# A fused dynamic convolution and token-routed MLP: a finer ring for x, and the selection of tokens in two rounds

## Chip, cores and metric

One core of one Trainium2 chip runs the whole program. The metric is the device time of one execution in microseconds (us); the profile adds a trace of one execution.

## What is computed

```python
# x (8, 4160, 192) fp32, weight_gen (8, 4160, 8 heads, 7 taps), capacity 128
w = exp(weight_gen - max over taps);  w = w / (sum over taps + 1e-9)
x_pad = 6 rows of zeros ahead of each batch of x
out[b, s, h] = sum over k of w[b, s, h, k] * x_pad[b, s + k, h]      # h: 24 columns
# then, for each batch b, on y = out:
scores = y[b] @ w_gate
top_idx = the 128 rows with the largest scores
xe = y[b, top_idx];  ye = relu(xe @ w1) @ w2                         # 192 -> 1024 -> 192
out[b, top_idx] = xe + sigmoid(scores[top_idx])[:, None] * ye
```

So there is a weighted sum of seven neighbouring rows with weights of its own for each row and head, and then a small MLP on the 128 best rows of each of the 8 batches, added back to those rows.

## The kernel before

The 33,280 rows are cut into tiles of 56 output rows (7 times 8), held on 64 partitions with the 6 rows ahead; two half ranges of a group of tiles share the 128 partitions. Four tiles are a pair (224 rows); there are NPR = 149 pairs and NS = 75 conv steps of two pairs each. A step is 32 matmuls (`conv`, L728), two halves by eight heads for each pair, with a banded 128x112 matrix as weights. VectorE builds that matrix (`band`, L707) from the transposed softmax weights, two steps ahead of its use, in NB = 3 buffers. ScalarE copies the sums out of PSUM one step later (`evac`, L742; two PSUM buffers `cps`), and SP's queue stores them.

The softmax weights come in NG = 5 groups of 32 pairs (16 steps): load, exp, sum, reciprocal, product (`sm_exp` to `sm_norm`, ScalarE and VectorE, in two halves of a group, the product at L242 and L252), then four transposes of quarters (`wt_t`, L267) whose copies (`wt_c`, L277 or L279) give `wts`. Where a batch begins inside a group, L252 multiplies by an edge mask that GpSimd makes (`edge_mask`, L796).

x lies in a ring of NX = 6 buffers of CP = 8 pairs (sixteen tiles on each partition half), loaded by GpSimd's queue (`load_x`, L166, two DMAs a piece; a buffer is loaded again when all its conv steps are emitted). The half of the buffer that holds no data must be zero, and GpSimd writes those zeros once (`zero_x`, L776 and L777).

The scores are not taken from the output: dot products of the rows of x with w_gate, head by head, are weighted by the softmax weights. A unit of eight tiles of x is transposed on TensorE (`y_unit_a`, L300, 24 instructions), copied by ScalarE and VectorE (`y_unit_c`, L308 and L309, tile `xT`), multiplied by `gmat` (`y_unit_b`, L321 to L327) and, piece by piece, cast to `y` by VectorE (`y_unit_d`, L335). There are 38 units, spread evenly over steps 0 to 57: unit k at step 58k/38, rounded down. After the last unit of a group `sc_moves` forms its scores (`score_t` to `score_r`; the product at L371 on VectorE, the sum by matmuls L386), writes them to DRAM (`sc_d`, L404) and reads back those of every batch that is complete (`scores`, L411), both on GpSimd's queue, which also carries the loads of x.

When the last group has its scores (about step 66), the selection runs once for all batches: candidates per partition (`sel_cand`), their values broadcast through DRAM (`cand_d` L481, `bc` L482), 24 rank counts, half on ScalarE and half on VectorE (`sel_rank`), 24 one-hot matrices on VectorE (`sel_hot`, L538) each with a matmul (L542), and the row numbers (`sel_fin`). Then GpSimd gathers the rows of all eight batches from the output in DRAM (`ex_gather`, L624), TensorE, ScalarE and VectorE run the MLP of one batch after another (`ex_k` to `ex_s`; the last operation is `ye`, L685), and GpSimd scatters each result (L690).

The order of all this is written out by hand in two lists per step: `reads` (emitted ahead of the step's matmuls) and `plan` (behind them). `at(s, f)` and `rd(s, f)` put a call there. Each engine works through its own instructions in that order, so an instruction that waits holds all that stand behind it on the same engine.

Of the kernel before, what the change touches and what calls it, by code (L numbers as in the profile page):

```python
# [18 lines left out]
P = 128  # L19
# [11 lines left out]
CP = 8  # L31
# [66 lines left out]
def fast_path(  # L98
# [18 lines left out]
    NX = 6  # L117
# [4 lines left out]
    wrb = [consts.tile([P, 4 * M, HK], FP32, name=f"wr{i}") for i in range(2)]  # L122
# [26 lines left out]
    def load_x(c):  # L149
        t = xb[c % NX].rearrange("p c k i d -> p c (k i) d")  # L150
        gi, l = divmod(c * CT, 2 * GP)
        for cc in range(2):
# [6 lines left out]
            while first + (hi - 1) * HB + R > N:  # L159
                hi -= 1  # L160
                f = first + hi * HB
                if f + K - 1 < N:
# [3 lines left out]
            nc.gpsimd.dma_start(  # L166
                out=t[R * cc:R * cc + R, cc, lo:hi, :],
                in_=ap_of(x_flat, x_flat.offset + (first + lo * HB) * D,
                          [[D, R], [HB * D, hi - lo], [1, D]]),
            )  # L170
# [117 lines left out]
    ybank = ps_y.tile([P, 2, CT, H], FP32, name="ybank")  # L288
    YT = 8
    YR = YT * D // P  # L290

    def y_unit_a(c, u):
        nr = min(YR, ntile(c) * D // P - u * YR)
        xf = xb[c % NX].rearrange("p c k i d -> p c (k i d)")
        tps = [ps_t.tile([P, 16, R], FP16, tag="tps", name=f"xtps{cc}") for cc in range(2)]
        for r in range(nr):
            for cc in range(2):
                ps = slice(R * cc, R * cc + R)
                o = (u * YR + r) * P
                nc.tensor.transpose(  # L300
                    out=tps[cc][:, r, :], in_=xf[ps, cc, o:o + P], identity=ident16[ps, ps]
                )
        ystate[(c, u)] = (tps, nr)

    def y_unit_c(c, u):
        tps, nr = ystate.pop((c, u))
# [3 lines left out]
        ystate[(c, u)] = xT  # L310

    def y_unit_b(c, u):
        nr = min(YR, ntile(c) * D // P - u * YR)
        nt = nr * P // D
        xT = ystate.pop((c, u))
        yps = ybank[:, c % 2, u * YT:u * YT + nt, :]
# [13 lines left out]
    def y_unit_d(c):  # L330
        nt = ntile(c)
        gi, l = divmod(c * CT, 2 * GP)
        if l == 0:
            ygr[gi] = ypl.tile([P, H, R], FP16, tag="y16", name="y16")
        nc.vector.tensor_copy(  # L335
            out=ygr[gi][:, :, l:l + nt].rearrange("p h t -> p t h"), in_=ybank[:, c % 2, 0:nt, :]
# [42 lines left out]
    def score_m(gi, odd):  # L379
        n = P  # L380
        sp = sps_.pop((gi, odd))
        if odd == 0:
            scs[gi] = ps_t.tile([P, 2, M // 2, Q, 8], FP32, tag="tps", name="sps")
        sps = scs[gi]
        for h in range(H):
            nc.tensor.matmul(  # L386
                out=sps[0:n, odd].rearrange("p m q k -> p m (q k)"), lhsT=ident16[0:n, 0:n],
                rhs=sp[0:n, :, h, :], start=(h == 0), stop=(h == H - 1), skip_group_check=True,
            )

    def score_r(gi):
        n = P
        sps = scs[gi]
        sc = smp.tile([P, Q, M // 2, 2], FP32, tag="sc", name="sc")
        nc.vector.tensor_reduce(  # L395
            out=sc[0:n].rearrange("p q m o -> p o m q"), in_=sps[0:n, :, :, :, 0:K],
            axis=AX.X, op=ALU.add,
        )
        parts = ((0, P, half_of(gi, 0, 0)),)
        if ntiles(gi) < R:  # L400
            parts = tuple((R * cc, ntiles(gi), half_of(gi, cc, 0)) for cc in range(2))
        for p0, n, h0 in parts:
            n = min(n, NHF - h0)
            nc.gpsimd.dma_start(  # L404
                out=sc_d[h0:h0 + n, :], in_=sc[p0:p0 + n].rearrange("p q m o -> p (q m o)")
            )
        beg = half_of(gi, 0, 0) * HB
        end = min(beg + 2 * ntiles(gi) * HB, N)
        for b in range(B):
            if beg < (b + 1) * S <= end:  # L410
                nc.gpsimd.dma_start(  # L411
# [23 lines left out]
    sel_i = selp.tile([P, B], I32, name="sel_i")  # L435
    gates = selp.tile([P, B], FP32, name="gates")
# [5 lines left out]
    def sel_consts():  # L442
        it = selp.tile([P, P], I32, name="it_i")
        nc.gpsimd.iota(out=it[:, :], pattern=[[1, P]], base=0, channel_multiplier=0)
        nc.gpsimd.tensor_copy(out=iota_f[:, :], in_=it[:, :])
# [34 lines left out]
    def sel_bcast():  # L480
        nc.gpsimd.dma_start(out=cand_d[:, :], in_=cv[:, :])  # L481
        nc.gpsimd.dma_start(  # L482
# [46 lines left out]
    def sel_hot(k):  # L529
        if k < ACT_K and k % 3 == 0:  # L530
            nc.vector.tensor_scalar(
                out=rank[:, k:k + 3], in0=rank[:, k:k + 3], scalar1=float(NR - 1), scalar2=0.5,
                op0=ALU.add, op1=MUL,
            )
        if k == 0:
            selst["ps"] = ps_t.tile([P, B, NV], FP32, tag="tps", name="lps")
        oh = ohp.tile([P, P], FP16, tag="oh", name="oh")
        nc.vector.tensor_scalar(  # L538
            out=oh[:, :], in0=iota_f[:, :], scalar1=rank[:, k:k + 1], scalar2=None,
            op0=ALU.is_equal,  # L540
        )
        nc.tensor.matmul(  # L542
            out=selst["ps"][:, :, :], lhsT=oh[:, :], rhs=rhs[:, k], start=(k == 0),
            stop=(k == CAND - 1),
        )

    def sel_fin():
        nc.scalar.copy(out=lists[:, :, :], in_=selst["ps"][:, :, :])
# [69 lines left out]
    NXE = B  # L618
    xebuf = [consts.tile([CAP, D], FP32, name=f"xe{i}_") for i in range(NXE)]

    def ex_gather(b):
        xe = xebuf[b % NXE]
        nc.gpsimd.memset(tick[:, :], 0.0)
# [58 lines left out]
    def ex_s(b):  # L682
        xe, yps = est[b][0], est[b][-1]
        ye = exq.tile([CAP, D], FP32, tag="ye", name="ye")
# [78 lines left out]
    nc.vector.memset(a_view(0)[:, :, :, K], 0.0)  # L763
    nc.vector.memset(amem[0][:, M * H * HB:], 0.0)
    nc.vector.memset(emax[:, :], 0.0)
    nc.vector.memset(rmax[:, :], 0.0)
# [8 lines left out]
    def zero_x(i):  # L775
        nc.gpsimd.memset(xb[i][R:P, 0], 0.0)  # L776
        nc.gpsimd.memset(xb[i][0:R, 1], 0.0)  # L777
# [26 lines left out]
    nc.gpsimd.tensor_copy(out=landed[:, 0:1], in_=wrb[0][:, 0, 0:1])  # L804
    load_x(0)
    zero_x(0)
    nc.gpsimd.tensor_copy(out=landed[:, 1:2], in_=wrb[1][:, 0, 0:1])
    load_x(1)
    load_x(2)
# [6 lines left out]
    zero_x(1)  # L816
    load_x(3)
    load_x(4)
# [14 lines left out]
    load_x(5)  # L833
    for i in range(3, NX):
        zero_x(i)
    sm_exp(0, 0)
# [29 lines left out]
    Y_END = 58  # L866
# [287 lines left out]
```

## Time and profile before

| | before |
|---|---|
| three runs | 289.55, 290.39, 288.17 us; median 289.55 |
| the profiled execution | 288.73 us, its span in the trace 286.9 us |
| busy: TensorE, VectorE | 173.8 us (61%), 184.7 us (64%) |
| busy: ScalarE, GpSimd | 149.6 us (52%), 108.3 us (38%) |
| mean granted TensorE clock | 0.747 of full speed |

Times below are us from the start of the span. PE is TensorE, PEld its weight load, DVE VectorE, ACT ScalarE, POOL GpSimd; GpSimd's DMA issues count as busy in its rows. A row of a table by stretch gives for each engine its busy time and, in brackets, the number of its instructions. The conv steps begin at 20.0 (step 0), 55.2 (step 8), 95.4 (step 20), 162.1 (step 42), 205.0 (step 56) and 229.0 (step 69); the first gather starts at 252.3.

### The profile page before, as it was taken

How to read it: one execution, taken by the hardware profiler on the slowest of the kernel's cores; microseconds unless marked ns; L12 is line 12 of the kernel's file. 1: busy time of each engine (PE TensorE's matmuls, PEld its weight loads, DVE VectorE, ACT ScalarE, POOL GpSimd, SP SyncE). 2: the span in 40 equal slices, each digit the busy share in tenths (PEclk: the TensorE clock that was granted, in tenths of full speed). 3: DMA queues.
4: the chain of work that ended last, by engine and by line, in shares of the span. 5: the costliest groups of instructions: out<-in, count | busy, mean ns of one | idle time of the engine just before them, and what ended most of it. 6: DMA issues, size and time to landing. Idle time of an engine off the chain costs nothing.

```text
span 286.9 us, 10859 instructions
## 1 busy us (share of the span) xinstructions
PE 173.8 (61%) x4759; PEld 158.4 (55%) x4759; DVE 184.7 (64%) x304; ACT 149.6 (52%) x234; POOL 108.3 (38%) x156
## 2 busy tenths in 40 slices
PE   0065480278667685777776894758978033738860
PEld 0065480178556684777676684748878032637740
DVE  4878050685648996456887753979797589824540
ACT  3527190077646497455676574686775129422420
POOL 5999999996020130203302030500103010077550
PEclk9999576556859959597555797768999855555996
DMA  6999995199999999998999999996487603342110
GB/s 224 201 232 211 221 210 152 6 180 238 228 287 275 250 162 232 186 280 260 200 236 176 265 170 219 142 240 188 112 227 212 196 29 99 98 114 76 43 45 17
DMA packets 78910, 51.22 MB, mean 179 GB/s; under 512 B 43402, under 2 KB 77181, under 8 KB 78858
## 3 DMA queue, kind: packets, MB, share of 16 engines
q0 software_dynamic: 41312, 17.44, 48.1%
q1 hardware_dynamic: 37546, 33.03, 39.8%
q8 instruction: 39, 0.64, 0.8%
q14 instruction: 13, 0.11, 0.1%
HBM read 39.35 MB, written 26.49 MB: 229 GB/s over the span
## 4 chain that ended last, share of the span: by engine, by line
PE 33%; issue 23%; POOL 17%; DVE 12%; DMA 10%; ACT 2%; POOLq 0%; DVEq 0%; ACTq 0%
PE cps L728 13%; POOL xb L776 6%; PE xtps L300 5%; POOL xb L777 5%; DMA xb<-in_x_dram 4%; POOL xb L166 4%; PE wtps L267 4%; DVE band L707 4%; DMA sc_d<-sc 4%; PE sps L386 3%; PE hps L661 3%; PE yeps L678 2%; DMA wr<-in_weight_gen_dram 2%; DVE amem L242 1%; DVE sp L371 1%
## 5 line engine op out<-in xcount | busy, mean ns | idle before, releaser
L728 PE MATMUL cps<-xb,band 128*128 128x48 f16 x2384 | 91.6, 199 | 44.1 <-DVE band L707 21.7
L728 PEld LDWEIGHTS <-band 128*128 128x128 f16 x2384 | 83.3, 107 | 48.8 <-issue 23.2
L707 DVE TENSOR_TENSOR band<-wts,mask 128x1792 f16<-128x1792 f16 (+1 forms) x75 | 83.4, 1124 | 2.7 <-PE cps L728 2.6
L742 ACT COPY co<-cps 112x768 f32<-112x768 f32 (+1 forms) x75 | 59.0, 792 | 48.4 <-PE cps L728 42.6
L166 POOL DMA_DIRECT2D xb<-in_x_dram x38 | 31.1, 829 | 57.3 <-PE cps L728 45.7
L309 DVE COPY xT<-xtps 128x768 f16<-128x768 f16 (+1 forms) x38 | 20.7, 545 | 42.5 <-PE xtps L300 28.2
L308 ACT COPY xT<-xtps 128x768 f16<-128x768 f16 (+1 forms) x38 | 29.9, 788 | 11.8 <-PE xtps L300 7.3
L300 PE MATMUL xtps<-ident,xb 64*128 64x64 f16 x894 | 26.9, 216 | 9.4 <-issue 7.1
L267 PE MATMUL wtps<-ident,amem 64*64 64x64 f16 x640 | 16.8, 214 | 18.2 <-DVE amem L242 13.9
L300 PEld LDWEIGHTS <-xb 64*128 64x128 f16 x894 | 20.9, 111 | 11.5 <-issue 7.8
L267 PEld LDWEIGHTS <-amem 64*64 64x64 f16 x640 | 15.0, 128 | 20.0 <-DVE amem L242 13.9
L279 ACT COPY wts<-wtps 128x1024 f16<-128x1024 f16 x18 | 18.3, 1015 | 13.8 <-PE wtps L267 13.7
L321 PE MATMUL ybank<-gmat,xT 128*128 128x8 f16 x149 | 15.4, 169 | 11.4 <-POOL gmat L828 6.2
L404 POOL DMA_DIRECT2D sc_d<-sc x6 | 3.4, 566 | 45.7 <-DVE sc L395 45.7
L242 DVE TENSOR_TENSOR amem<-amem,r 128x2048 f16<-128x2048 f16 (+1 forms) x10 | 10.9, 1093 | 13.4 <-POOL edge L796 13.3
L210 ACT ACTIVATE amem<-wr 128x1792 f16<-128x1792 f32 (+1 forms) x10 | 15.2, 1515 | 7.4 <-DVE amem L252 3.7
L324 PEld LDWEIGHTS <-xT 128*128 128x128 f16 x149 | 12.8, 102 | 11.2 <-issue 11.2
L221 DVE TENSOR_REDUCE den<-amem 128x256 f32<-128x1792 f16 (+1 forms) x10 | 17.7, 1776 | 1.6 <-ACT amem L210 1.6
L777 POOL MEMSET xb<- 64x3072 f16 x6 | 15.9, 2652 | 0.3
L776 POOL MEMSET xb<- 64x3072 f16 x6 | 15.9, 2653 | 0.2
L324 PE MATMUL ybank<-gmat,xT 128*128 128x16 f16 x149 | 15.3, 172 | 0.6 <-POOL gmat L828 0.6
L335 DVE CAST y<-ybank 128x128 f16<-128x128 f32 (+1 forms) x19 | 13.6, 717 | 3.1 <-PE ybank L327 2.9
(164 smaller groups left out, 254.2 us busy)
## 6 DMA issues: line engine op xcount, KB each, us to landing
out_dram<-co SPq DMA_DIRECT2D x148, 168.0 KB, 5.8
xb<-in_x_dram POOLq DMA_DIRECT2D x35, 384.0 KB, 10.0
wr<-in_weight_gen_dram SPq DMA_DIRECT2D x4, 896.0 KB, 5.8
wr<-in_weight_gen_dram SPq DMA_DIRECT2D x4, 672.0 KB, 4.2
wr<-in_weight_gen_dram SPq DMA_DIRECT2D x2, 224.0 KB, 6.9
w_sb<-in_moe_w_dram POOLq DMA_DIRECT2D x1, 384.0 KB
xb<-in_x_dram POOLq DMA_DIRECT2D x1, 360.0 KB
wr<-in_weight_gen_dram SPq DMA_DIRECT2D x2, 168.0 KB
```

Of the source, the lines that this page charges most:

```text
L166: nc.gpsimd.dma_start(out=t[R * cc:R * cc + R, cc, lo:hi, :], in_=ap_of(x_flat, x_flat.offset + (first + lo * HB) * D, [[D, R], [HB * D, h ...
L267: nc.tensor.transpose(out=tp[ps, hh, m, :], in_=am[ps, o:o + R], identity=ident16[ps, ps])
L279: nc.scalar.copy(out=dst, in_=src)
L300: nc.tensor.transpose(out=tps[cc][:, r, :], in_=xf[ps, cc, o:o + P], identity=ident16[ps, ps])
L308: nc.scalar.copy(out=xT[:, 0:nr, 0, :], in_=tps[0][:, 0:nr, :])
L309: nc.vector.tensor_copy(out=xT[:, 0:nr, 1, :], in_=tps[1][:, 0:nr, :])
L324: nc.tensor.matmul(out=yps[:, 2 * q:2 * q + 2, :], lhsT=lhs, rhs=gmat[:, 1:3, :], start=False, stop=False, skip_group_check=True)
L707: nc.vector.tensor_tensor(out=bandbuf[si % NB][:, HB:HB + NSLOT * SL].rearrange("p (s z q m) -> p s z q m", z=2, q=Q, m=M)[:, 0:ns, 0], in ...
L728: nc.tensor.matmul(out=dst[:, :, h * G:(h + 1) * G], lhsT=bt[:, o:o + P], rhs=xb[c % NX][:, :, k, i, h * G:(h + 1) * G], start=(i == 0 and ...
L742: nc.scalar.copy(out=co[0:SL, 0:np_].rearrange("p j c d -> p j (c d)"), in_=cps[0:SL, 0:np_, 0:2 * D])
L776: nc.gpsimd.memset(xb[i][R:P, 0], 0.0)
L777: nc.gpsimd.memset(xb[i][0:R, 1], 0.0)
```

## The change

The ring gets thirteen buffers of four pairs (eight tiles on each half). A unit of dot products is now a whole piece, and unit c stands at step max(c, 2c - 19): one per step up to step 19, every second step after that; the cast follows every second unit. In the prologue GpSimd's zeros are written as fp32 words (half the elements), ScalarE writes those of buffer 0, the two pad memsets of `amem[1]` go to VectorE, the constants `gmat` and the edge masks of all batches come between the loads of x or right behind the last of them. The softmax of groups 1 to 4 starts at steps 2, 16, 28 and 42 (before at 2, 18, 34 and 46), the scores of groups 0 to 3 at steps 11, 22, 34 and 50.

`sc_d`, `scores`, `cand_d` and `bc` are issued by ScalarE instead of GpSimd, the read one step behind the write. The score sums are reduced half by half. The selection runs twice: round 0 behind the scores of group 2, at steps 42 to 55, two rank counts of each engine a step, with the one-hot matmuls in six PSUM groups that VectorE adds up; then the gathers of batches 0 to 4 at step 57 and their MLPs from step 58 on, one every two steps. Round 1 follows the scores of the last group, three rank counts a step, and batches 5 to 7 go through the MLP after it. Each round works on all eight batches.

```diff
-CP = 8
+CP = 4
-    NX = 6
+    NX = 13
...
     def score_s(gi):
...
-            nc.gpsimd.dma_start(
+            nc.scalar.dma_start(
                 out=sc_d[h0:h0 + n, :], in_=sc[p0:p0 + n].rearrange("p q m o -> p (q m o)")
             )
+
+    def score_l(gi):
...
-                nc.gpsimd.dma_start(
+                nc.scalar.dma_start(
                     out=scores[b * PPB:(b + 1) * PPB, :].rearrange("p (j r) -> p j r", r=BLK),
...
-    def sel_hot(k):
...
+    def sel_hot(ks):
+        k0, k1 = ks[0], ks[-1] + 1
...
+        ps = ps_t.tile([P, B, NV], FP32, tag="tps", name="lps")
+        both = [*ks, *(ACT_K + k for k in ks)]
+        for k in both:
+            oh = ohp.tile([P, P], FP16, tag="oh", name="oh")
...
+    def sel_sum(first):
+        if first:
+            nc.vector.tensor_copy(out=lists[:, :, :], in_=selst["ps"][:, :, :])
+        else:
+            nc.vector.tensor_tensor(
+                out=lists[:, :, :], in0=lists[:, :, :], in1=selst["ps"][:, :, :], op=ALU.add
+            )
...
     def zero_x(i):
-        nc.gpsimd.memset(xb[i][R:P, 0], 0.0)
-        nc.gpsimd.memset(xb[i][0:R, 1], 0.0)
+        for cc in range(2):
+            p0 = R * (1 - cc)
+            v = xb[i][p0:p0 + R, cc].rearrange("p k i d -> p (k i d)").bitcast(FP32)
+            if i == 0:
+                nc.scalar.copy(out=v, in_=emax[p0:p0 + R, 0:1].to_broadcast([R, CT * D // 2]))
+            else:
+                nc.gpsimd.memset(v, 0.0)
...
+    for gi, s in ((1, 2), (2, 16), (3, 28), (4, 42)):
+        sm_moves(gi, s)
+    for gi, s in enumerate((11, 22, 34, 50)):
+        e = sc_moves(gi, s)
+        if gi == 2:
+            ea = sel_moves(0, e + 2, 2)
+    at(14, sel_consts)
+    at(20, load_experts)
...
+    for b in range(LATE):
+        ex_moves(b, ea + 1, ea + 3 + 2 * b)
+    eb = sel_moves(1, sc_moves(NG - 1, ydone[NG - 1] + 1) + 2, 3)
```

GpSimd's order around `gmat` before: `xb_103` and so on are the buffers of the ring, the memsets their zeros, `gsel` and `gmat` the constants of the dot products.

```order
L807 COPY landed<-wr_109 128x1
L166 DMA xb_103<-in_x_dram 64x16x192 x2
L166 DMA xb_104<-in_x_dram 64x16x192 x2
L776 MEMSET xb_103 64x3072
L777 MEMSET xb_103 64x3072
L166 DMA xb_105<-in_x_dram 64x16x192 x2
L166 DMA xb_106<-in_x_dram 64x16x192 x2
L776 MEMSET xb_104 64x3072
L777 MEMSET xb_104 64x3072
L823 AFFINE_SELECT gsel<-wcol 128x8
L828 AFFINE_SELECT gmat<-gsel 128x8
```

The same place in the change, on the same engine:

```order
L167 DMA xb_103<-in_x_dram 64x8x192 x2
L803 MEMSET xb_103 64x768 x2
L841 COPY landed<-wr_116 128x1
L167 DMA xb_104<-in_x_dram 64x8x192 x2
L167 DMA xb_105<-in_x_dram 64x8x192 x2
L167 DMA xb_106<-in_x_dram 64x8x192 x2
L167 DMA xb_107<-in_x_dram 64x8x192 x2
L803 MEMSET xb_104 64x768 x2
L848 AFFINE_SELECT gsel<-wcol 128x8
L853 AFFINE_SELECT gmat<-gsel 128x8
```

Ahead of `gmat` stand four memsets of 768 words (two buffers) in place of six of 3072 elements (three buffers, the first above this piece). The six edge masks of the change stand behind the last load of the ring (buffer 12) and ahead of ten more memsets, where before four of them stood behind all memsets.

VectorE at steps 48 to 50 before (`band` of the step two ahead, the softmax of group 4, `xT` and `y` of the dot products):

```order
L707 TENSOR_TENSOR band_116<-wts_113,mask 128x32x56
L309 COPY xT<-xtps_4255 128x12x64
L707 TENSOR_TENSOR band_114<-wts_113,mask 128x32x56
L242 TENSOR_TENSOR amem_110<-amem_110,r_4281 128x64x32
L252 TENSOR_TENSOR amem_110<-amem_110,edge 128x64x8
L335 CAST y_3569<-ybank 128x16x8
L707 TENSOR_TENSOR band_115<-wts_113,mask 128x32x56
```

And in the change, the same three steps (L530 the rank counts, L547 the one-hot matrices, `lps` their sums from TensorE):

```order
L727 TENSOR_TENSOR band_123<-wts_120,mask 128x32x56
L243 TENSOR_TENSOR amem_117<-amem_117,r_4383 128x64x24
L530 TENSOR_SCALAR junk,rank<-bc,cv 128x384 x2
L727 TENSOR_TENSOR band_121<-wts_120,mask 128x32x56
L530 TENSOR_SCALAR junk,rank<-bc,cv 128x384 x2
L539 TENSOR_SCALAR rank<-rank 128x2
L547 TENSOR_SCALAR oh<-iota_f,rank 128x128 x4
L335 CAST y_4566<-ybank 128x16x8
L309 COPY xT<-xtps_4484 128x12x64
L559 COPY lists<-lps 128x40
L727 TENSOR_TENSOR band_122<-wts_120,mask 128x32x56
```

Between one `band` and the next now stand rank counts, one-hots and the sums of the list, which before stood behind step 66.

ScalarE around the first score write in the change (`co` the copies out of PSUM, L211 the exp of the next group); before, neither `sc_d` nor `scores` stood on this engine:

```order
L762 COPY co<-cps 112x768
L308 COPY xT<-xtps_1885 128x12x64
L211 ACTIVATE amem_117,emax<-wr_115 128x4x64x7
L407 DMA sc_d<-sc 128x56
L762 COPY co<-cps 112x768
L308 COPY xT<-xtps_1977 128x12x64
L416 DMA scores<-sc_d 16x13x20
L762 COPY co<-cps 112x768
```

GpSimd held them before, between its loads of x:

```order
L166 DMA xb_106<-in_x_dram 64x16x192 x2
L404 DMA sc_d<-sc 128x56
L411 DMA scores<-sc_d 16x13x20 x2
L166 DMA xb_107<-in_x_dram 64x16x192 x2
L166 DMA xb_102<-in_x_dram 64x10x192
```

The read of `scores`, which follows `sc_d` through DRAM, has moved from a queue between loads of x to the engine that empties PSUM, with one copy `co` and one `xT` between write and read.

## Rows read from the trace of the kernel before

**Rows 1.** Stretches: start:end, length, busy PE, PEld, DVE, ACT, POOL, clock, DMA.
```profile
20.00:55.20 35.20, 15.63 (x448) 14.54 (x449) 14.00 (x16) 13.03 (x19) 34.51 (x31) 0.72 1.09 170
55.20:95.40 40.20, 28.49 (x832) 26.59 (x832) 28.23 (x36) 23.28 (x32) 16.00 (x37) 0.69 1.25 229
95.40:162.10 66.70, 49.69 (x1443) 46.04 (x1438) 49.75 (x60) 42.51 (x64) 12.20 (x16) 0.67 1.14 220
162.10:205.00 42.90, 30.96 (x1008) 28.48 (x1004) 30.17 (x37) 28.94 (x41) 6.95 (x10) 0.84 0.93 192
205.00:229.00 24.00, 15.06 (x509) 14.08 (x501) 18.18 (x29) 13.19 (x18) 3.39 (x6) 0.95 0.73 208
229.00:252.30 23.30, 10.99 (x200) 9.29 (x200) 20.12 (x75) 12.21 (x32) 1.37 (x4) 0.50 0.26 73
252.30:286.90 34.60, 19.33 (x210) 15.84 (x210) 11.60 (x34) 7.95 (x17) 17.58 (x31) 0.75 0.20 59
```
**Rows 2.** Waits between 20 and 55.2: total us, times, longest.
```profile
PEld L728 <- DVE band L707: 14.3, 2, 11.7
DVE amem L242 <- POOL edge L796: 13.3, 1, 13.3
PE ybank L321 <- POOL gmat L828: 6.2, 1, 6.2
```
**Rows 3.** Groups of GpSimd's instructions by line, and its timeline: start, us.
```profile
L776 POOL MEMSET xb<- 64x3072 f16 x6 | 15.9, 2653 | 0.2
...
5.87 0.25 POOL L156 MEMSET xb<- 6x192 f16 x1
52.49 2.75 POOL L796 TENSOR_SCALAR_AFFINE_SELECT edge<-tri 128x64 f16<-128x64 f16 x4
186.02 0.71 POOL L166 DMA_DIRECT2D xb<-in_x_dram  x1
```
**Rows 4.** Memsets of GpSimd, groups by line: total us, mean ns.
```profile
L610 POOL MEMSET w_b<- 64x1024 bf16 x1 | 0.9, 946 | 0.1
L448 POOL MEMSET xe__152<- 128x192 f32 x1 | 0.3, 257 | 0.0
```
**Rows 5.** Transposes L300 alone by stretch: PE, PEld, clock, DMA, GB/s.
```profile
55.20:95.40 40.20, 5.31 (x192) 4.28 (x192) 0.69 1.25 229
162.10:205.00 42.90, 6.41 (x216) 4.76 (x216) 0.84 0.93 192
```
**Rows 6.** Tile xT alone: PE, PEld, DVE, ACT, clock, DMA, GB/s.
```profile
55.20:95.40 40.20, 3.69 (x96) 3.29 (x96) 4.96 (x9) 6.41 (x8) 0.69 1.25 229
```
**Rows 7.** Conv matmuls L728 alone, by stretch: PE, PEld, clock, DMA, GB/s.
```profile
55.20:95.40 40.20, 15.56 (x384) 13.94 (x384) 0.69 1.25 229
205.00:229.00 24.00, 11.93 (x416) 11.26 (x416) 0.95 0.73 208
229.00:252.30 23.30, 8.07 (x176) 7.41 (x176) 0.50 0.26 73
```
**Rows 8.** The selection by stretch, all engines, then VectorE's L707 in the first.
```profile
225.10:252.30 27.20, 10.99 (x200) 9.29 (x200) 23.85 (x85) 12.21 (x32) 1.37 (x4) 0.53 0.30 86
235.00:251.50 16.50, 7.95 (x136) 6.63 (x136) 14.62 (x57) 12.00 (x30) 0.00 (x0) 0.50 0.31 85
...
225.10:252.30 27.20, 6.02 (x6) 0.53 0.30 86
```
**Rows 9.** GpSimd's timeline of the tail: start, us, then idle before and releaser.
```profile
265.22 1.00 POOL L690 DMA_INDIRECT out_dram<-ye,sel_i  x1 [1.25 <-DVE ye L685]
267.45 0.98 POOL L690 DMA_INDIRECT out_dram<-ye,sel_i  x1 [1.10 <-DVE ye L685]
```
**Rows 10.** Waits of the whole span; the chain of waits; GpSimd's timeline.
```profile
POOL scores L411 <- DMA sc_d<-sc: 24.6, 5, 10.1
...
168.11 10.43 DMA sc_d<-sc
220.58 1.15 POOL L411 DMA_DIRECT2D scores<-sc_d  x2 [1.97 <-DMA sc_d<-sc]
```

## What the change is predicted to do

> **What bounds the kernel now.** I cut the run into stretches by conv steps and read busy times of all engines in each [rows 1]: no engine is at its peak over the whole, so each stretch has its own bound. In the opening (20.0 to 55.2, steps 0 to 7) GpSimd is busy 34.51 of 35.2 us while TensorE does 15.63 and VectorE 14.00. The waits there [rows 2] say whom it holds: TensorE stands 6.2 us for `gmat`, VectorE 13.3 us for an edge mask, and through VectorE's delayed `band` TensorE another 11.7 us. GpSimd has nothing hard to do; it writes zeros, 2.65 us each, twelve in all (both lines, six each) [rows 3].
>
> From step 8 to 56 TensorE is the busiest (28.49 of 40.2, 49.69 of 66.7, 30.96 of 42.9) with VectorE next to it or level (28.23, 49.75, 30.17). In the end of the conv (229.0 to 252.3) VectorE is the bound: 20.12 of 23.3 us. In the heart of the selection it is busy 14.62 of 16.5 us, 89% [rows 8]. I take that 89% as what a VectorE-bound stretch of this program reaches. Behind the first gather no engine is full (TensorE 19.33 of 34.6): the scatters come 267.45 - 265.22 = 2.23 us apart, each held by `ye` [rows 9], so this is a chain per expert.
>
> **The opening.** GpSimd's load of x keeps its bytes, so its zeros decide. Half the elements, in a wider type, is not in the trace. Bounds: the 64x1024 bf16 memset takes 0.946 us, 0.71 for 768 elements by elements, and by words (1536 of bf16) at most 1.42; the 128x192 fp32 memset of 0.257 us gives 1.03 for four times its width [rows 4]. I take 0.75, so a buffer costs 1.5 instead of 5.3. A DMA issue of eight tiles is priced by the 0.71 of the smaller loads [rows 3]. GpSimd is ready at 5.9 [rows 3]; a small memset and five issues for buffers 0 and 1 (0.3 + 3.6), 1.5 of zeros, 0.2 of copy, eight issues (5.7), 1.5 of zeros put `gmat` at 5.9 + 12.8 = 18.7, ahead of step 0. Its eight tiny instructions take 2 at the 0.25 of the small memset [rows 3]. Then come zeros (1.5), eight issues (5.7), zeros (1.5), three times 1.4 + 1.5, and the six masks (2.75 for four, some of it waiting, so about 3 [rows 3]): 18.7 + 2 + 8.7 + 8.7 + 3 = 41. Before, the masks began at 52.49. If they come at 41, the 6.2 and 11.7 of TensorE's waits go, 17.9 together, and two more units of dot products come in: eight steps have eight where the spread had six. VectorE then has 14.00 + 1.8 (two copies and a cast) + 1.5 (softmax of group 1, earlier) = 17.3, at 89% 19.5 us; the mask holds it to about 21. So the opening is 21 instead of 35.2: **-14**. Bound above: each load of x may stand for the landing of an earlier one, then GpSimd is as late as before and the term is 0; half of that is -6.
>
> **Steps 8 to 20.** 12 units in place of 8. A unit costs TensorE 5.31/8 + 3.69/8 = 1.12 us [rows 5, 6]: +4.5. Against that, TensorE no longer comes out of an 11.7 us stall into steps at the lower clock: its clock in this stretch is 0.69, and steps take 15.56/384 x 32 = 1.30 us [rows 7] where they take 11.93/416 x 32 = 0.92 at clock 0.95; if ten of the twelve steps gain 0.38 it is -3.8. **+1**, range -2 to +6.
>
> **Steps 20 to 42.** 11 units instead of 14 (-3.4), three weight quarters (32 transposes each at 5.31/192 [rows 5], +2.7) and half a group's scores come in (product and sum over 1792 elements, each as a `band` of that size, 6.02/6 = 1.0 [rows 8], +2): **+1**.
>
> **Steps 42 to 56.** Here round 0 lies between the `band`s. A round's price on VectorE: 225.1 to 252.3 holds 23.85 us, of it 6.02 for six `band`s [rows 8], so 17.8. The list's five sums and the copy come on top (1.3), two dot-product units go (-1.1): 30.17 + 17.8 + 1.3 - 1.1 = 48.2, at 89% 54 us for 42.9: **+11** (8 to 14). TensorE has 30.96, fewer dot products, and the one-hot matmuls, less than the 7.95 that it did in the selection's heart [rows 8]: not the bound. ScalarE gets 12 rank counts (12.2 us is all it does in the selection's stretch [rows 1]) on 28.94: 41 of 54. The cover that the rank counts had before, a VectorE that was the bound alone, is what moves.
>
> **Steps 56 to 69.** Five experts. An expert's share of the last stretch is 19.33/8 = 2.42 us of TensorE and 11.60/8 = 1.45 of VectorE [rows 1]. TensorE: 15.06 + 12.1 = 27.2. VectorE: 18.18 + 7.25 + 3.3 (candidates and values of round 1, earlier) = 28.7, at 89% 32.3 us for 24.0: **+8.3** (4 to 12). The gathers wait for the stores of batches 0 to 4, long issued; GpSimd has nothing else queued behind them but the scatters.
>
> **Steps 69 to the gather.** The candidates' 3.3 are gone, the sums cost about 1.3: **-2** (-3 to +1).
>
> **The tail.** Five experts fewer at 2.23 us: **-11.2**.
>
> Sum: -14 + 1 + 1 + 11 + 8.3 - 2 - 11.2 = -5.9, against the profiled execution of 288.73 (span 286.9 and 1.83 around it): 282.8. The median of the runs shown is 0.8 above the profiled one: **283.6**.
>
> **The queue of the scores.** `sc_d` now is issued by ScalarE, and the read waits one step later; behind it stand the next `co` and `xT`, for which TensorE waits. On GpSimd the write took 10.43 us to land in steps with x loads, and the read waited 24.6 us in five times; with no x left to load it waited 1.97 [rows 10]. I take the landing as near 2 to 4 us, because the loads of x are then in another queue, and cost the move at nothing: a step of 66.7/22 = 3.0 us lies between write and read. The other end is the landing that GpSimd saw: (10.1 + 0.6 - 3.0) = 7.7, none for the 1.97, and three of 4.2 + 0.6 - 3.0 = 1.8: 13 us. The Trainium skill, page "DMA: Bandwidth & Descriptors", section "Issuing engines are not separate DMA queues", speaks for that end: transfers started by different engines run on the same 16 DMA engines and interleave, and starting them elsewhere saves only the sequencer's time to start them. By it the sum would be 296, by the row of 1.97 it is 283.6; the trace so far has both, since the 10.43 fell in a stretch whose DMA column is 0.93 and the 1.97 in one of 0.73 [rows 1].
>
> **The rivals.** *TensorE's clock stays high.* The granted clock is 0.69 and 0.67 in steps 8 to 42 (a mixture of the two levels, 1.2 and 2.4 GHz) and 0.95 in steps 56 to 69 [rows 1]; without the opening's stall and with denser steps it might stay up. The 34 steps there would cost 0.92 in place of 1.30: -12.9; the other 34 us of TensorE work (28.49 + 49.69 - 34 x 1.30) get half of the same share off, -5; of it 3.8 is counted above: 269.5. Against it: before, the stretch from 95 to 162 had no such stall in front and was at 0.67. *The clock stays low*, 1.2 GHz throughout as after 229.0 (0.50): steps of 8.07/176 x 32 = 1.47 [rows 7], 0.17 more, +5.8; the other work in proportion, +4.4; the 3.8 lost: 297.6, slower than before. It decides once TensorE, not VectorE, ends the steps. *ScalarE stands for the scores*, as worked out: 296; it decides where the landing takes over two steps, 6 us, since TensorE has two `cps` buffers. *The opening is not freed*, the change not doing what it says there: the loads hold GpSimd, masks come past 50: 283.6 + 13 = 297.
>
> **How the numbers follow.** The forecast 0.50 (its own range 276 to 291, from the terms' bounds taken together), the high clock 0.18, the low clock 0.13, ScalarE's wait 0.11, the opening 0.08. A measurement of this kernel can tell about 1% from no change: under 286.7 is faster, over 292.4 slower. The forecast's range lies about two thirds under the first and hardly over the second: 0.32 + 0.18 = 0.50 faster; 0.15 of the forecast and 0.07 of half-sized rivals make 0.22 same; 0.28 slower. Low end 269 (half of the high-clock case is left out, 0.09), high end 299 (about 0.08 left out).
>
> **What would show it.** In the new trace: no wait for `gmat`, masks by 41, step 8 at about 41; step 20 about 82, step 42 about 150, step 56 about 204; VectorE busy near 89% from 42 to 69; steps 56 to 69 in 32 us; step 69 about 236, the gather of batch 5 at about 258 and three experts in about 23 us behind it; ScalarE's wait between `sc_d` and `scores` near nothing. The forecast is wrong if VectorE has holes in steps 42 to 69 (a wait of the rank counts for `bc`, or of `lists` for TensorE), if the experts in the conv wait for their gathers, or if the clock of steps 8 to 42 leaves 0.6 to 0.75.

## The result, and the profile after

The changed kernel takes 280.41 us in the median (278.37 to 283.0, four runs) against 289.69 for the kernel before: a ratio of 0.966 (0.958 to 0.975). The forecast was 283.6 in a range of 269 to 299. The total is near; several of its terms are not, and the experiments show that one part of the change, the first round of the selection, takes back what the others bring.

The profile shown is a second execution of the same kernel (278.8 us of span); the first, at 281.2 us and a lower mean clock (0.706 against 0.747), differs from it in no stretch by more than 3 us. First the stretches (start:end, length, busy TensorE, its weight load, VectorE, ScalarE, GpSimd with counts, granted clock, DMA engines' busy share, GB/s), the answer to [rows 1]:

```profile
20.20:43.50 23.30, 17.48 (x521) 16.29 (x522) 19.10 (x22) 16.13 (x25) 19.90 (x31) 0.67 1.38 216
43.50:88.50 45.00, 32.00 (x978) 29.40 (x977) 28.68 (x40) 25.21 (x34) 26.24 (x53) 0.73 1.28 222
88.50:156.20 67.70, 48.16 (x1436) 44.46 (x1433) 47.79 (x60) 41.29 (x61) 19.13 (x30) 0.78 1.20 226
156.20:209.20 53.00, 34.84 (x867) 31.87 (x867) 44.88 (x116) 32.84 (x61) 5.26 (x9) 0.60 0.65 147
209.20:238.90 29.70, 22.73 (x585) 20.75 (x584) 26.05 (x54) 16.58 (x28) 13.53 (x18) 1.00 0.63 179
238.90:259.80 20.90, 10.16 (x202) 8.16 (x199) 18.84 (x72) 12.60 (x31) 1.66 (x3) 0.61 0.47 132
259.80:278.80 19.00, 7.96 (x80) 6.37 (x80) 5.11 (x19) 2.96 (x7) 6.48 (x11) 0.68 0.12 35
```

Against the forecast, in us:

| steps | before | forecast | the change | one selection (below) |
|---|---|---|---|---|
| 0 to 8 | 35.2 | 21 | 23.3 | 21.6 |
| 8 to 20 | 40.2 | 41 | 45.0 | 45.5 |
| 20 to 42 | 66.7 | 68 | 67.7 | 67.1 |
| 42 to 56 | 42.9 | 54 | 53.0 | 34.4 |
| 56 to 69 | 24.0 | 32 | 29.7 | 23.2 |
| 69 to the gather | 23.3 | 21 | 20.9 | 21.2 |
| the gather to the end | 34.6 | 23 | 19.0 | 30.9 |

Of the opening's waits [rows 2] little is left: none for the mask, none of the dot products for `gmat`, and 2.7 us for the first `band`, ahead of step 0. GpSimd's masks begin at 43.81, 2.8 us later than worked out; two of the loads ahead of them stood 2.6 us together for the landing of an earlier one (a DMA has landed when its data are in place). GpSimd's timeline (start, us, then idle before and its releaser, the one that ended the wait):

```profile
41.62 0.68 POOL L167 DMA_DIRECT2D xb<-in_x_dram  x1 [1.69 <-DMA xb<-in_x_dram]
42.34 1.52 POOL L803 MEMSET xb<- 64x768 f32 x2
43.81 2.75 POOL L822 TENSOR_SCALAR_AFFINE_SELECT edge<-tri 128x64 f16<-128x64 f16 x6
```

Two memsets of 768 words take 1.52 us together: 0.76 each, as estimated (0.75).

In the tail, as [rows 9], three gathers come ahead of the first scatter. Of GpSimd's timeline the first gather and the three scatters:

```profile
259.80 1.04 POOL L643 DMA_INDIRECT xe__161<-out_dram,sel_i  x1 [16.70 <-DVE gates L578]
...
267.98 1.02 POOL L710 DMA_INDIRECT out_dram<-ye,sel_i  x1 [4.43 <-DVE ye L705]
...
270.22 0.99 POOL L710 DMA_INDIRECT out_dram<-ye,sel_i  x1 [1.13 <-DVE ye L705]
...
272.45 0.99 POOL L710 DMA_INDIRECT out_dram<-ye,sel_i  x1 [1.16 <-DVE ye L705]
```

The first gather, the first and the last scatter of the kernel before:

```profile
252.26 1.12 POOL L624 DMA_INDIRECT xe__152<-out_dram,sel_i  x1 [19.83 <-DVE gates L560]
...
262.82 1.03 POOL L690 DMA_INDIRECT out_dram<-ye,sel_i  x1 [0.22 <-issue]
...
278.66 0.97 POOL L690 DMA_INDIRECT out_dram<-ye,sel_i  x1 [1.18 <-DVE ye L685]
```

### The profile page after: what moved, and what is told of

The parts are those of the page before. It is cut to its first block, busy times and chain, and to the rows that moved or that the text cites. A ratio compares the mean times of both kernels' runs of the same rounds, so it can differ in the third digit from the quotient of the medians.

```text
span 281.2 us, 11054 instructions
## 1 busy us (share of the span) xinstructions
PE 181.1 (64%) x4783; PEld 165.1 (59%) x4783; DVE 203.7 (72%) x404; ACT 158.4 (56%) x260; POOL 108.9 (39%) x185
## 4 chain that ended last, share of the span: by engine, by line
PE 36%; issue 21%; DVE 20%; DMA 5%; ACT 4%; ACTq 0%; POOL 0%; POOLq 0%; DVEq 0%
PE cps L748 15%; DVE band L727 6%; PE xtps L300 5%; PE sps L385 4%; PE wtps L268 4%; DMA sc_d<-sc 3%; DVE junk L530 2%; ACT co L762 2%; PE hps L680 2%; PE yeps L697 1%; DVE den L222 1%; DVE amem L243 1%; PE ybank L324 1%; DMA xe__161<-out_dram,sel_i 1%; DVE oh L547 1%
## 5 line engine op out<-in xcount | busy, mean ns | idle before, releaser
L748 PEld LDWEIGHTS <-band 128*128 128x128 f16 x2384 | 85.9, 108 | 40.0 <-issue 28.8
L167 POOL DMA_DIRECT2D xb<-in_x_dram x75 | 51.1, 699 | 87.8 <-PE cps L748 44.2
L727 DVE TENSOR_TENSOR band<-wts,mask 128x1792 f16<-128x1792 f16 (+1 forms) x75 | 80.2, 1078 | 0.4 <-PE cps L748 0.3
L309 DVE COPY xT<-xtps 128x768 f16<-128x768 f16 (+1 forms) x38 | 23.2, 611 | 16.3 <-PE xtps L300 8.5
L300 PE MATMUL xtps<-ident,xb 64*128 64x64 f16 x894 | 27.7, 222 | 5.1 <-issue 5.1
L268 PE MATMUL wtps<-ident,amem 64*64 64x64 f16 x640 | 18.6, 223 | 18.7 <-DVE amem L243 14.1
L300 PEld LDWEIGHTS <-xb 64*128 64x128 f16 x894 | 21.9, 115 | 6.3 <-issue 5.5
L643 POOL DMA_INDIRECT xe__161<-out_dram,sel_i x2 | 2.1, 1075 | 48.8 <-DVE gates L578 48.8
L710 POOL DMA_INDIRECT out_dram<-ye,sel_i x8 | 10.9, 1368 | 23.4 <-DVE ye L705 23.4
L321 PE MATMUL ybank<-gmat,xT 128*128 128x8 f16 x149 | 15.6, 169 | 6.2 <-DVE xT L309 3.1
L211 ACT ACTIVATE amem<-wr 128x1792 f16<-128x1792 f32 (+1 forms) x10 | 15.2, 1518 | 6.8 <-DVE amem L253 4.7
L803 POOL MEMSET xb<- 64x768 f32 x24 | 17.6, 732 | 1.1
L551 PE MATMUL lps<-rhs,oh 128*128 128x40 f16 x48 | 7.8, 213 | 14.5 <-DVE oh L547 14.0
L327 PE MATMUL ybank<-gmat,xT 128*128 128x8 f16 x149 | 15.4, 167 | 1.5 <-issue 1.5
```

What stands on the lines that cost most here:

```text
L167: nc.gpsimd.dma_start(out=t[R * cc:R * cc + R, cc, lo:hi, :], in_=ap_of(x_flat, x_flat.offset + (first + lo * HB) * D, [[D, R], [HB * D, h ...
L268: nc.tensor.transpose(out=tp[ps, hh, m, :], in_=am[ps, o:o + R], identity=ident16[ps, ps])
L300: nc.tensor.transpose(out=tps[cc][:, r, :], in_=xf[ps, cc, o:o + P], identity=ident16[ps, ps])
L309: nc.vector.tensor_copy(out=xT[:, 0:nr, 1, :], in_=tps[1][:, 0:nr, :])
L321: nc.tensor.matmul(out=yps[:, 2 * q, :], lhsT=lhs, rhs=gmat[:, 0, :], start=True, stop=False, skip_group_check=True)
L727: nc.vector.tensor_tensor(out=bandbuf[si % NB][:, HB:HB + NSLOT * SL].rearrange("p (s z q m) -> p s z q m", z=2, q=Q, m=M)[:, 0:ns, 0], in ...
```

## The experiments

Every kernel ran beside the kernel before on the same chip, and ratios are to that. There were three sets on three chips, with medians of 288.8, 290.5 and 291.2 us for the kernel before, so times are compared within a set. The second set (more stores, wider spread, bands on GpSimd, one selection on GpSimd's queue) had no run of the change; it is compared by ratios and by the profiles of the other sets.

**The same kernel twice more**, the measure for the first and the third set.

> The changed kernel once more, unchanged, as the measure for the runs beside it and for a second profile. Its first profiled execution took 283.0 us at a mean granted clock of 0.706 and spent 47.6 us on steps 8 to 20, where the prediction had 41. Theory A: those 6.4 us belong to that execution's clock (0.64 there); a profile at a mean clock near 0.745 shows steps 8 to 20 in 41 to 43 us and an end near 279. Theory B: they belong to the change (twelve units of dot products on TensorE in place of eight); steps 8 to 20 take 46 to 48 us at any clock. All else as in the first profile: opening 23 us, steps 20 to 42 68, 42 to 56 54, 56 to 69 30, first gather of batch 5 to the end 18.5.

281.08 us, ratio 0.975 (0.967 to 0.984). Steps 8 to 20 took 45.0 us at a clock of 0.73, where the first profile had 0.64: most of the excess over the forecast belongs to the change, not to the clock.

> The changed kernel unchanged, beside the next run on the same chip: 279 to 282.

284.54 us, ratio 0.983 (0.976 to 0.990); its profile had a stall that the other had not (last section).

**The opening alone**, put into the kernel before:

```diff
+    zero_x(0)
     load_x(0)
-    zero_x(0)
...
     load_x(1)
-    load_x(2)
+    zero_x(1)
...
+    zero_x(2)
+    load_x(4)
     load_x(5)
+    for b in range(2, B):
+        edge_mask(b)
     for i in range(3, NX):
         zero_x(i)
```

with `zero_x` and the pad memsets as in the change.

> The kernel before with the opening of the change alone (zeros as fp32 words, ScalarE zeroing buffer 0, pad memsets on VectorE, gmat and all edge masks between the loads; ring of six sixteen-tile buffers, one selection, scores on GpSimd's queue as before). GpSimd reaches the masks at about 27 us in place of 52. My term: the opening is 14 us shorter, of which the changed kernel showed 12.2, and nothing gives it back: 289.7 - 12 to 14 = 276 to 278. Rival: what the opening gains is given back in steps 8 to 56, where TensorE and its clock are the bound (denser steps at the lower clock): step 8 comes 12 earlier but step 56 less than 6, and the time is 283 or more.

277.51 us, ratio 0.961 (0.952 to 0.970), 11.2 less than before, and 3.6 less than the whole change in the same set. So in this set the opening alone is worth at least as much as everything together. Its stretches to step 56:

```profile
20.30:39.10 18.80, 15.49 (x449) 14.52 (x450) 17.31 (x19) 14.26 (x23) 16.93 (x20) 0.84 1.43 220
39.10:82.70 43.60, 31.03 (x834) 28.71 (x832) 25.18 (x33) 22.59 (x29) 12.79 (x32) 0.62 1.34 243
82.70:145.40 62.70, 46.16 (x1441) 42.18 (x1437) 48.25 (x59) 42.06 (x64) 12.21 (x16) 0.80 1.19 227
145.40:194.90 49.50, 35.66 (x1008) 32.51 (x1004) 31.16 (x39) 29.39 (x41) 6.94 (x10) 0.69 0.97 182
```

The opening is 16.4 shorter than before; step 42 comes 16.7 earlier, and steps 42 to 56 give 6.6 back.

**One move of it**, the masks ahead of the last zeros:

```diff
     load_x(5)
+    for b in range(2, B):
+        edge_mask(b)
     for i in range(3, NX):
         zero_x(i)
...
-    for b in range(2, B):
-        at(1 + b // 2, edge_mask, b)
```

> The kernel before with one move: the edge masks of batches 2 to 7 come behind the last load of the ring and ahead of the zeros of buffers 3 to 5 (at about 35 us in place of 52). TensorE's 11.7 us behind band go, the 6.2 for gmat stay. Theory of the prediction (TensorE's waits are the price): step 8 at 43.5 in place of 55.2, and the time 278 to 280. Rival, the DMA engines: GpSimd still writes zeros to 51 and starts no load before, so the loads of the second ring come no earlier; the steps gained are given back behind step 8, and the time is 284 or more.

289.33 us, ratio 1.000 (0.995 to 1.004): nothing. Both theories of the expectation missed why. The masks came at 34.61, but VectorE's wait only changed its name; this is a row of the waits between 20 and 60 (us in total, times, longest):

```profile
DVE amem L242 <- POOL amem L910: 14.5, 1, 14.5
```

And two of GpSimd's timeline:

```profile
34.61 1.17 POOL L796 TENSOR_SCALAR_AFFINE_SELECT edge<-tri 128x64 f16<-128x64 f16 x6
...
53.57 0.41 POOL L910 MEMSET amem<- 128x8 f16 x1
```

The product at L242 needs the pads of `amem`, which GpSimd wrote here at 51.91 to 53.98. It does not read the mask at all; only L252 behind it does. In the kernel before the pads end at 52.85, 0.03 us ahead of the product, with the masks right behind them on GpSimd, so the view, which names what came last, put the 13.3 us [rows 2] down to a mask. GpSimd and VectorE before:

```profile
50.78 2.07 POOL L907 MEMSET amem<- 128x448 f16 x1
52.44 0.41 POOL L908 MEMSET amem<- 128x8 f16 x1
...
52.88 1.23 DVE L242 TENSOR_TENSOR amem<-amem,r 128x2048 f16<-128x2048 f16 x1 [13.29 <-POOL edge L796]
```

The change moves both, so its term held. Whether the opening's gain is TensorE's waits or the transfers that could not start, this run does not decide.

**One selection** in the changed kernel, all experts behind it:

```diff
-        e = sc_moves(gi, s)
-        if gi == 2:
-            ea = sel_moves(0, e + 2, 2)
+        sc_moves(gi, s)
...
-    for b in range(LATE):
-        ex_moves(b, ea + 1, ea + 3 + 2 * b)
```

with `LATE = 0`, so that batches 0 to 7 go through the loop behind round 1.

> The changed kernel with one selection, behind the scores of the last group, and all eight experts behind it (round 0 and the early experts left out; three of the eight gather buffers lie in x buffers that are free by then). By the terms as the first profile of the change has them (steps 42 to 56 +10.9, 56 to 69 +5.7, 69 to the gather -2.3, tail -16.1, together -1.8) it takes 282, within 2 us of the change: two rounds are worth nearly nothing. By my prediction's terms (+11, +8.3, -2, -11.2, together +6.1) it takes 274 to 275, 6 us less than the change. Rival: the tail is worth more than the profile's stretches show, then it takes 286 or more.

268.59 us, ratio 0.932 (0.920 to 0.944), 12.5 less than the change by the medians; its four runs lie between 265.93 and 273.43. All three expectations were too high. Steps 42 to 56 and 56 to 69, then the tail:

```profile
154.40:188.80 34.40, 26.85 (x846) 25.48 (x842) 26.83 (x32) 25.10 (x37) 5.26 (x9) 0.80 1.02 224
188.80:212.00 23.20, 15.17 (x459) 14.40 (x453) 20.85 (x34) 11.25 (x17) 0.00 (x0) 0.93 0.71 197
...
233.20:264.10 30.90, 17.73 (x210) 14.24 (x210) 11.51 (x34) 7.65 (x17) 17.40 (x31) 0.83 0.19 54
```

VectorE's busy time from 42 to 56 is 44.88 with round 0 and 26.83 without: 18.05, where the forecast charged 17.8 + 1.3 = 19.1 for the round. But the stretch without it takes 34.4, not 42.9.

> The kernel with one selection once more, with more rounds, since it is the fastest so far: 266 to 271, 10 to 14 us under the changed kernel of the same rounds.

273.77, ratio 0.951 (0.944 to 0.957), 10.8 less than the changed kernel in this set. It beats both kernels in both sets.

**Round 0 kept, its experts moved** behind round 1. Their gathers are moved too, but GpSimd has nothing queued ahead of them and their row numbers are ready, so five of them still run from 207.15 on, at step 57:

```diff
-    for b in range(LATE):
-        ex_moves(b, ea + 1, ea + 3 + 2 * b)
...
-    for i, b in enumerate(range(LATE, B)):
+    for i, b in enumerate(range(B)):
```

> The changed kernel with both selections in place, but the five early experts moved behind round 1, so that all eight stand at the end, as with one selection (three gather buffers lie in free x buffers). It splits the 12.5 us that two rounds cost (281.1 against 268.6) into round 0's own work and the early experts. By the profiles of the two kernels: steps 42 to 56 keep their 53 us, 56 to 69 fall from 29.7 to about 23, the gather to the end grows from 19.0 to 31: 281 - 6.5 + 11.9 = 286. My prediction's terms would say 281 - 7.25/0.89 + 11.2 = 284. Rival: the early experts cost more than they save, 280 or less.

288.84 us, ratio 1.001 (0.995 to 1.006). In the same set the change has 284.54 and one selection 273.77: round 0 itself costs 15.1, and the early experts bring back 4.3. The sum of the experts' two terms in the forecast, +8.3 - 11.2 = -2.9, had the right sign and about the right size.

**The transfers of the scores on GpSimd's queue again**:

```diff
-            nc.scalar.dma_start(
+            nc.gpsimd.dma_start(
                 out=sc_d[h0:h0 + n, :], in_=sc[p0:p0 + n].rearrange("p q m o -> p (q m o)")
             )
```

and so with `scores`, `cand_d` and `bc`.

> The changed kernel with the four score transfers (sc_d, scores, cand_d, bc) issued by GpSimd again, in the same places of the order. My theory: on ScalarE they cost nothing (the first profile shows ScalarE standing 3.7 us once behind sc_d), on GpSimd the read waits behind the write as before (24.6 us in five waits) and holds the loads of x that stand behind; with thirteen buffers there is slack for that, so the time is the same within 1% (279 to 282). Rival 1: the held loads make TensorE wait for x, 283 to 290. Rival 2: ScalarE's waits were a cost, then this is faster by 2 to 4 us.

292.04 us, ratio 1.012 (1.004 to 1.020), 11.0 more than the change: rival 1, and beyond its range. Its waits over the whole span:

```profile
POOL scores L416 <- DMA sc_d<-sc: 26.9, 4, 12.3
PEld L300 <- DMA xb<-in_x_dram: 6.9, 5, 2.5
ACT junk L525 <- DMA bc<-cand_d: 6.9, 1, 6.9
```

GpSimd's timeline in round 1:

```profile
244.86 0.62 POOL L487 DMA_DIRECT2D cand_d<-cv  x1
...
249.43 1.58 POOL L710 DMA_INDIRECT out_dram<-ye,sel_i  x1 [3.89 <-DVE ye L705]
251.01 0.69 POOL L490 DMA_DIRECT2D bc<-cand_d  x1
```

GpSimd stands 26.9 us for `sc_d`, TensorE now waits for x, and the broadcast is queued behind the scatter of an early expert that itself waits for its `ye`: 6.15 us from `cand_d` to `bc`, where the change has 236.38 to 237.86 on ScalarE. That second wait exists only because experts now scatter during round 1. By the two profiles the stretches from step 8 to 56 are 4.1 us longer than in the change, 56 to 69 by 3.9 and 69 to the gather by 4.3, so the stretches in which x is loaded carry a part of the price and not most of it. How it divides among the four transfers, which moved together, no run tells.

> The kernel with one selection (268.6) with the four score transfers issued by GpSimd, between its loads of x, as in the kernel before. Theory: the queue is what made steps 42 to 56 fall from 43.0 to 34.4 and it is worth as much here as with two rounds (292.0 against 281.1): 278 to 281, with GpSimd waiting 25 us or so for sc_d, steps 42 to 56 at 41 to 43, and TensorE waiting for x. Rival: the 11 us come from waits that only two rounds have (the second broadcast, round 0 in the x stage): then 270 to 273.

With one selection the same edit took 277.26 us, ratio 0.948 (0.938 to 0.958), in another set than one selection on ScalarE's queue (0.932 and 0.951), so its price there stays open: nothing to 5 us by the ratios, 8 by the two profiles that have the same stall (277.3 and 269.3 of span). Steps 42 to 56 took 35.5 us, so the queue alone does not bring them back to 42.9, as I had expected. That does not clear the queue: in the kernel before a landing of 10.43 us lies in this stretch [rows 10], and in the new order the writes of the scores lie outside it (150.55 and 192.07, where the stretch is 156.4 to 191.9). One selection also has less work in the stretch than the kernel before (VectorE 26.83 us for 30.17, TensorE 26.85 for 30.96, ScalarE 25.10 for 28.94). Which of these makes the fall, no run tried.

**What bounds steps 8 to 42.** One more store in each step, into a scratch tensor:

```diff
+                if cc == 1 and 8 <= si < 42:
+                    nc.sync.dma_start(
+                        out=ap_of(extra, extra.offset + t0 * D,
+                                  [[D, SL], [SL * D, full], [1, D]]),
+                        in_=co[0:SL, 0:full, cc, :],
+                    )
```

> The changed kernel with one more store in each of steps 8 to 41: half of what the step stores (224 rows of 768 bytes) is stored a second time into a scratch tensor, 5.85 MB in all, issued by SP; no engine but SP has more to do. Theory A, TensorE and its clock end the steps from 8 to 42, as the prediction had it: steps 8 to 42 take what they took (112.7 us in the second profile), within 4. Theory B, the DMA engines end them (216 to 226 GB/s in every stretch to step 42 in every kernel so far): they take 5.85 MB / 225 GB/s = 26 us more, or 20 by the time that the queue's packets took; 133 to 139 us, and 300 to 306 in all.

296.23 us, ratio 1.019 (1.008 to 1.030). Steps 8 to 20 and 20 to 42:

```profile
42.40:90.40 48.00, 34.23 (x978) 31.60 (x976) 29.73 (x43) 25.38 (x34) 28.71 (x56) 0.64 1.29 239
90.40:165.50 75.10, 50.08 (x1435) 46.57 (x1433) 47.38 (x58) 41.48 (x61) 17.95 (x29) 0.73 1.27 253
```

123.1 us where the change has 112.7 (the other profiles of the new order have 110.3 to 115.3): 10.4 more for transfers alone, about half of the 20 to 26 that a hard limit of the DMA engines would give, and far from the nothing of a TensorE bound. They also moved more per us than before, up to 253 GB/s. The kernel ran twice, at 296.29 and 296.16. SP's queue stood 40 us here for its own earlier stores, where it stood 7 in the change, so whether the price is the DMA engines' or this queue's is not shown.

> The changed kernel with units 8 to 22 of the dot products spread wider (two fewer in steps 8 to 20, the rest shifted one to four steps back); the score places stay. TensorE theory of the prediction (1.12 us of TensorE for a unit): steps 8 to 20 get 2 to 4 us shorter and 20 to 42 as much longer. DMA theory: neither moves by more than the 2 us between profiles, except as x buffers come free later. Both: the time is the same within 1%, 279 to 283.

The edit puts units 11 to 27 one to four steps later than `max(c, 2 * c - 19)`, so that steps 8 to 20 have nine units and not twelve. Steps 8 to 20 took 43.9 and 20 to 42 69.2, 1.1 less and 1.5 more than in the change; at 1.12 us a unit TensorE's theory has 3.4 for each. The whole took 284.84 us, ratio 0.982 (0.973 to 0.991); 5.6 us more than in the second profile of the change lie in steps 56 to 69 (the stall), none before.

**Bands on GpSimd**, with one selection, to relieve VectorE:

```diff
-        nc.vector.tensor_tensor(
+        eng = nc.gpsimd if si % 2 and si >= 44 else nc.vector
+        eng.tensor_tensor(
```

> The kernel with one selection, and every second band from step 45 on (15 in all) built by GpSimd instead of VectorE; GpSimd has 5.3 us of work in steps 42 to 56 and none in 56 to 69. Theory: in steps 56 to 69 and from 69 to the gather VectorE is the bound (20.85 of 23.2, 19.0 of 21.2), so taking 6 + 3 bands of 1.0 us off it gives 5 to 8 us, if GpSimd needs less than two steps (4 us) for a band: 261 to 264. Steps 42 to 56 keep their 34 (DMA engines). Rival: GpSimd is slow or holds VectorE up while it works: 268 or more.

288.24 us, ratio 0.988 (0.976 to 0.999), 11 to 20 more than one selection without it, by ratios or medians. GpSimd needs 3.2 us and more for a band, and VectorE's own work got slower: in steps 56 to 69 it is busy 23.85 us with 7 bands, where it had 20.85 with 14 (last section). A row of GpSimd's timeline:

```profile
179.53 3.23 POOL L731 TENSOR_TENSOR band<-wts,mask 128x1792 f16<-128x1792 f16 x1 [2.29 <-PE cps L752]
```

And the stretch of steps 56 to 69:

```profile
193.30:225.90 32.60, 19.19 (x451) 17.77 (x452) 23.85 (x27) 11.29 (x17) 22.47 (x7) 0.67 0.48 132
```

## Why the prediction was right, and where it was not

**The opening: held.** -14 forecast, -11.9 in the profile, -11.2 us in all for the opening alone. The price of the zeros was right (0.76). The loads' waits for landings (the bound that I had named) cost 2.6 us. The reading of [rows 2] was lucky: VectorE's 13.3 us were a wait for the pads and not for the mask, and the change happened to move the pads too.

**Steps 8 to 42: the sum is off by 4, and its reason does not carry it.** I costed them by TensorE's instructions, +1 and +1; they took +4.8 and +1.0. Three units of dot products moved 1.1 and 1.5 us where that price says 3.4, and transfers, at which the sum does not look, moved 10.4. Nor does the granted clock set the sum: 112.6 us at 0.62 and 0.77 (one selection), 112.7 at 0.73 and 0.78 (the change). So neither clock rival came about, though the 0.78 lies outside the 0.6 to 0.75 beyond which I had called the forecast wrong. I had the row that pointed elsewhere, the DMA column of 1.25 and 1.14 with 229 and 220 GB/s [rows 1], and read past it. The bound itself stays open. Besides the transfers there are gaps of TensorE for which the view finds no releaser ("issue"): 23.9 us of the 112.7, and before 23.5 of 106.9. The row of steps 20 to 42:

```profile
PE cps L748 <- issue: 10.5, 5, 3.8
```

**Steps 42 to 56: right by +11 against +10.1, and yet mis-sized.** The round's own work was priced well (19.1 against 18.05 us of VectorE). What failed is the step in which I took 42.9 us as what the stretch takes without it: one selection takes 34.4. Against that, round 0 costs 15 us in the whole kernel and 18.6 in this stretch, not 11. Nor is the stretch VectorE's work at 89%: it is busy 44.88 of 53.0 us (85%), not 48.2 of 54, and more than half of the rest is one hole of 5.9 us (4.5 of them behind step 42), of the kind that I had named as a sign of being wrong. Round 0's first instruction stands there for the `scores` (the view names a store as releaser, but the instruction reads `scores`), with `band`s behind it:

```profile
DVE cv L479 <- DMA out_dram<-co: 5.9, 1, 5.9
```

The forecast compared each stretch with the kernel before, so it could not see that two parts of the change compete for the same time.

**Steps 56 to 69: +5.7 against +8.3**, with VectorE at 88% of the stretch as said; its work was 26.05, not 28.7, since not all that I had counted there lies there: the fifth expert's scatter is at 241.44, behind step 69 (238.9). With the stall it is 35.3, +11.3.

**The tail: mis-sized, -15.6 against -11.2.** I took 2.23 us per expert [rows 9]. The five fewer scatters are that, 11.4 (7 x 2.26 of spacing before, 2 x 2.24 after). Unseen were the gathers: GpSimd issues all of them ahead of the first scatter, which before came 10.56 us behind the first gather (released by nothing but GpSimd itself) and now 8.18: -2.4. From the last scatter's issue to the end it is 6.35 instead of 8.24, another -1.9. In every profile with the scores on GpSimd's queue this last piece is 7.8 to 8.4, in every one with them on ScalarE's 6.3 to 6.5; why is open.

**The queue of the scores: the step that failed most.** I costed the move at nothing, with ScalarE's wait as the only rival, and named no gain. With two rounds the move is worth 11.0 us. The bound on the loss was asked for (+13) and the bound on the gain not, though [rows 10] had it: GpSimd's 24.6 us in front of its own loads. The landing was wrong too: I took 2 to 4 us because the loads of x are in another queue. From the issue of `sc_d` to the read, which waits for it, the change takes 5.8, 5.4 and 6.5 us for the three writes that fall among the loads of x (77.55 to 83.34, 114.34 to 119.71, 147.81 to 154.27) and 2.5 at 209.54, behind the last of them. So the wait that the rival named did come. The view of waits shows little of it:

```profile
ACT co L762 <- DMA sc_d<-sc: 5.5, 2, 4.1
```

The 4.1 us of this row end with TensorE's sums, at 117.5, ahead of the landing, which the read saw at 119.7. Behind two other reads ScalarE stands 4.24 and 5.54 us more, which the view labels "issue" because the read, and not the copy, did the waiting. ScalarE's timeline:

```profile
147.81 0.34 ACTq L407 DMA_DIRECT2D sc_d<-sc  x1
...
154.27 1.00 ACTq L416 DMA_DIRECT2D scores<-sc_d  x2
155.37 1.50 ACT L762 COPY co<-cps 112x768 f32<-112x768 f32 x2 [5.54 <-issue]
```

With the other 1.4 us of the row that is about 11 us of ScalarE against the 13 that I gave the rival. After the read at 154.27 TensorE stood 3.1 us for a `co`, and the 5.9 us hole of steps 42 to 56 ends with the same scores. The move paid in spite of this, since on GpSimd's queue the same write took 9.1 us in the median to land and held loads, gathers and scatters.

The rule of the Trainium skill that I had set against the move (page "DMA: Bandwidth & Descriptors", section "Issuing engines are not separate DMA queues"), that issuing elsewhere saves only the sequencer's time to start a transfer, does not describe this kernel: the move was worth 11.0 us, and what the traces show behind them is not the time to start transfers but waits that stood in GpSimd's sequence, between loads and scatters.

So the total came out 3 us from the forecast by errors of both signs, which is luck: steps 8 to 42 too low by 3.8 and the opening by 2.1, the tail too high by 4.4 and steps 56 to 69 by 2.6. The queue's gain and the shorter steps 42 to 56 lay unpriced behind round 0, which used them up.

## What to carry to other kernels

Price a part of a change against the kernel with the other parts in, not against the kernel before: idle time that one part is costed into may be what another part would have freed, and then one of them should be dropped (here one selection instead of two, 268.6 against 281.1). When a waiting DMA issue moves to another queue, bound the gain by what stood behind it on the old queue, as carefully as the loss on the new one, and look at the issue that waits, not only at the engine's waits. Before an engine is named the bound of a stretch, look at the share of the DMA engines in the same row and at the gaps without a releaser. Before a wait's releaser is moved, check that the waiting instruction reads what the releaser writes.

## What the runs showed of the hardware that I had not expected

In seven of the fourteen profiles, the changed kernel's third among them and not its first two, VectorE stands for 3.4 to 4.1 us while GpSimd issues the gathers, with no releaser in the program. In the four of them in which the gathers fall into conv steps, TensorE meanwhile issues its matmuls three or four at a time with up to 0.5 us between. Whole kernels differ by it: steps 56 to 69 of the change took 35.3 us with it and 29.7 without. From the third profile, VectorE:

```profile
212.37 0.24 DVE L656 CAST xh__166<-xe__161 128x192 bf16<-128x192 f32 x1
216.59 1.09 DVE L727 TENSOR_TENSOR band<-wts,mask 128x1792 f16<-128x1792 f16 x1 [3.97 <-remote]
```

TensorE meanwhile:

```profile
215.06 0.26 PE L748 MATMUL cps<-xb,band 128*128 128x48 f16 x4 [0.51 <-issue]
```

Its cause is open; no run tried it.

The other surprise is GpSimd as a helper for VectorE: the same product takes 1.0 us on VectorE [rows 8] and 3.2 and more on GpSimd, and it costs VectorE time while it runs. From the kernel with bands on GpSimd, two products of VectorE, the first within GpSimd's two bands of 199.89 to 207.18 and the second outside, then a search for candidates within the five of 214.14 to 232.75:

```profile
204.00 4.12 DVE L372 TENSOR_TENSOR sp<-amem,Y 128x1792 f16<-128x1792 f16 x1
209.93 1.09 DVE L372 TENSOR_TENSOR sp<-amem,Y 128x1792 f16<-128x1792 f16 x1 [1.80 <-PE sps L385]
...
218.35 0.43 DVE L479 MAX8 cv<-scores 128x8 f32<-128x260 f32 x1
```

The first product is 3.0 us longer than the second, which is about one band of GpSimd; the search takes the 0.43 us that it takes without them.
